# Scaled queries and keys on their way through DRAM: the four rows of a feature side by side, in place of four separate blocks

## The chip, the cores and the metric

The kernel runs on one core of one Trainium2 chip. Its time is the device time of one execution in microseconds. Three runs of the kernel before took 1242.01, 1244.40 and 1241.99 us; their median, 1242.01 us, is the number that the change is compared with.

## The reference, cut to what matters

```python
def _attn_ref(q, k, v, a_re, a_im):           # 4 batches, 8 heads, 768 steps, 48 features
    mag = np.sqrt(a_re * a_re + a_im * a_im)
    scale = np.minimum(mag, 0.999) / (mag + 1e-06)
    a_re_n, a_im_n = (a_re * scale, a_im * scale)
    for t in range(S):
        new_re = ar * S_re - ai * S_im
        new_im = ar * S_im + ai * S_re
        S_re, S_im = (new_re + k_t (outer) v_t, new_im)
        y[:, :, t] = q_t @ S_re
def _moe_ref(x, ...):    # 3072 tokens, 384 -> 1536 -> 384
    g = x @ w_gate
    return (g / (1 + np.exp(-g)) * (x @ w_val)) @ w_out
def _moe2_ref(x, ...):   # 384 -> 2048 -> 384
    h = x @ w_in
    return (h - np.tanh(h)) @ w_out
```

A recurrence with a complex decay per feature and step is followed by two feed-forward layers. All inputs of the first part are float32; the weights of the two layers are float64.

## The kernel before, in words

The recurrence is done in 24 units of 128 steps (4 batches, 6 pieces each), two units to a group. `group_steps` builds the products of the decays of a group (the tile `PL`, by chains of `cstep` on VectorE), writes them as factors into `NW`, and passes the group's last products through DRAM (`lam_d`). In front of it, `put_a` transposes the decays on TensorE into the PSUM tile `psA`, of which there is one, and ScalarE copies that into `PL` and `A0`.

`unit_a` (L367 to L402) prepares one unit. It transposes queries and keys on TensorE (`psQ`, L377), so that a partition is a feature: 3 blocks of 128 features (index j) by 128 steps. VectorE multiplies both with the real and the imaginary factors (L386) into the tile `QK`. For each of 384 features there are then four rows of 128 float32: i is 0 for the query and 1 for the key, c is 0 for the real and 1 for the imaginary factor. The scores need another grouping: for each head, 96 partitions, the 48 features of the head with the real factor and then the same 48 with the imaginary one. Getting there means moving data between partitions, and the kernel does it by way of DRAM: one write of `QK` to `qk_d` (L388), then four reads (L393): two for the keys into the tile `TK`, two for the queries into `TQ`. The four rows of a feature lie in four separate blocks of `qk_d`, 384 x 128 numbers each, so every piece that lies together in DRAM and in SBUF alike is one row: 512 bytes.

`unit_b` (L412 to L483) finishes a unit: scores `psS` from `TK` and `TQ` (L430), masked into `SC`; the state `psG` to `Z` and `Hn`, with a swap of two halves by DMA (`Zs`); the output `psY` from `SC` and, in all but the first unit of a batch, from `Hn` and `TQ` (L458, L462); and its copies into `x`, which are the tokens of the first layer. `window` interleaves `unit_b` of one unit with `unit_a` of the next.

The first layer runs in ten token tiles of two or three units (`moe1_tile`): matmuls of gate and value weights (L574), Silu on ScalarE (L578), a product and a split into two parts on VectorE (L583, L534), and the matmuls back (L558). `bg` calls let the recurrence of the following units run between its steps. Its float64 weights are loaded (L181 to L187) into two buffers `raw` and taken apart by `words` (L144 to L148) while the first tile runs. The second layer (`moe2_tile`) follows after all units are done.

Within each engine, the order of the program is set by the framework's scheduler when the kernel is built: it plays the program through with its own durations and places every instruction. All DMAs are issued by one queue, SyncE's, in that order: a DMA whose input is not ready holds up those behind it. `QK` and `TK` have one buffer (`bufs=1`), and so has `TQ` by its pool.

Of the kernel before, what the change touches and what calls it, by code (L numbers as in the profile page):

```python
# [8 lines left out]
F32 = mybir.dt.float32  # L9
# [4 lines left out]
ALU = mybir.AluOpType  # L14
# [3 lines left out]
P = 128  # L18
# [23 lines left out]
def tile_kernel(ctx: ExitStack, tc: tile.TileContext, q, k, v, a_re, a_im, w_gate, w_val, w_out, w2_in, w2_out, out):  # L42
    nc = tc.nc
    PE, ACT, DVE, POOL, SP = nc.tensor, nc.scalar, nc.vector, nc.gpsimd, nc.sync
    B, H, S, D = q.shape
    NT, DM = out.shape
# [3 lines left out]
    NJ = DM // P  # L50
    D2 = 2 * D
    G = 2
    units = [(b, c) for b in range(B) for c in range(NC)]
    NU = len(units)
# [19 lines left out]
    dram = ctx.enter_context(tc.tile_pool(name="scratch", bufs=1, space=DRAM))  # L74


    ident = const.tile([P, P], F32, name="ident")
# [20 lines left out]

    wo_d = dram.tile([NF1, P, 2, DM], F32, name="wo_d")
    lam_d = dram.tile([NU // G, DM, 3, G], F32, name="lam_d")  # L100
    qk_d = dram.tile([NU, 2, 2, DM, P], F32, name="qk_d")
    o_d = dram.tile([P, 2, NJ, NT], F32, name="o_d")
    x_d = dram.tile([NT, DM], F32, name="x_d")

# [3 lines left out]
    a1 = att.enter_context(tc.tile_pool(name="a1", bufs=1, side="right"))  # L108
# [23 lines left out]
    def PA(name):  # L132
        pool, tag = banks[0]
        banks.append(banks.pop(0))
        return pool.tile([P, 512], F32, tag=tag, name=name)

    def heads(x):
        return x.rearrange("p (h d) -> p h d", h=H)
# [228 lines left out]
    def unit_a(u):  # L367


        qn, kn = st.pop(("q", u)), st.pop(("k", u))  # L370
        NW, LS, g = st["w", u]
        W = [NW[:, c, g] for c in range(3)]
        qk = a1.tile([P, 2, NJ, P], F32, tag="qk", name="qk")
        for i, x in enumerate((qn, kn)):
            ps = PA("psQ")
            for j in range(NJ):
                PE.transpose(ps[:, P * j:P * (j + 1)], x[:, P * j:P * (j + 1)], ident)  # L377
            p = ps[:, 0:DM].rearrange("p (j t) -> p j t", j=NJ)
            near, far = (slice(0, HALF), slice(HALF, P))[::1 - 2 * i]
            DVE.tensor_tensor(out=qk[:, i, :, near], in0=p[:, :, near], in1=W[2][:, :, near], op=ALU.mult)  # L380
            ACT.copy(out=qk[:, i, :, far], in_=p[:, :, far])
            yield
        QK = a1.tile([P, 2, 2, DM], F32, tag="QK", name="QK", bufs=1)
        sh = [P, 2, DM]
        for i in range(2):
            DVE.tensor_tensor(out=QK[:, i], in0=qk[:, i].rearrange("p j t -> p (j t)").unsqueeze(1).to_broadcast(sh), in1=NW[:, 0:2, g].rearrange("p c j t -> p c (j t)"), op=ALU.mult)  # L386
        d = qk_d[u]
        SP.dma_start(out=d.rearrange("i c (j p) t -> p i c j t", p=P), in_=QK.rearrange("p i c (j t) -> p i c j t", j=NJ))  # L388
        TK = a1.tile([D2, H, P], F32, tag="TK", name="TK", bufs=1)
        TQ = a1.tile([D2, H, P], F32, tag="TQ", name="TQ")  # L390
        for i, x in ((1, TK), (0, TQ)):
            for c in range(2):
                SP.dma_start(out=x[c * D:(c + 1) * D], in_=d[i, c].rearrange("(h d) t -> d h t", h=H))  # L393
        yield
        Kn = a1.tile([P, H, 2, D], F32, tag="Kn", name="Kn")
        for c in range(2):
            ps = PA("psK")
            for j in range(NJ):
                PE.transpose(ps[:, P * j:P * (j + 1)], QK[:, 1, c, P * j:P * (j + 1)], ident)
            ACT.copy(out=Kn[:, :, c, :], in_=heads(ps[:, 0:DM]))  # L400
            yield
        st["u", u] = (Kn, TK, TQ)  # L402

# [8 lines left out]
    def unit_b(u):  # L412
        b, c = units[u]
        NW, LS, g = st["w", u]
        Kn, TK, TQ = st["u", u]
        vn = vp[u % 2]
# [10 lines left out]
        for hh in range(2):  # L427
            ps = PA("psS")
            for i in range(4):
                PE.matmul(ps[:, P * i:P * (i + 1)], lhsT=TK[:, 4 * hh + i], rhs=TQ[:, 4 * hh + i], start=True, stop=True)  # L430
            t = a1.tile([P, 4, P], F32, tag=f"SC{hh}", name="SC")
# [23 lines left out]
        for i in range(H // 2):  # L455
# [3 lines left out]
            if c > 0:  # L459
                for h in (2 * i, 2 * i + 1):  # L460
                    r = HALF * (h % 2)
                    PE.matmul(ps[r:r + D, i], lhsT=Hn[:, D * h:D * (h + 1)], rhs=TQ[:, h], start=False, stop=True)  # L462
        y = a1.tile([P, 4, 2, P], F32R, tag="y", name="y")
# [21 lines left out]
    def window(b, a):  # L485
        first = a == 1

        b = unit_b(b) if b is not None else iter(())
        a = unit_a(a) if a is not None else iter(())

        for s_ in (a, a, a, b, b, b, b, b, a, a) if first else (a, b, b, a, a, b, a, b, a, b):
            if next(s_, 0) is None:
                yield
        for s_ in (b, a):
            for _ in s_:
                yield
# [284 lines left out]
    with tc.If(bad > 0):  # L781
        with ExitStack() as gen:
# [12 lines left out]
            with tc.For_i(0, q.shape[2], TB) as t0:  # L795
# [40 lines left out]
                for i in range(2):  # L836
                    ps = PA("psY")[0:B * H, 0:n * D]
# [5 lines left out]
        with ExitStack() as gen:  # L843
# [14 lines left out]
            with tc.For_i(0, NT, P) as t0:  # L858
# [3 lines left out]
                ps = PA("psX")  # L862
# [4 lines left out]
                for f in range(NF1):  # L867
                    ps = []
                    for w in (gw, vw):
                        p = ps_1.tile([P, 512], F32, tag="l1", name="l1")[:, 0:P]  # L870
# [6 lines left out]
                for j in range(NJ):  # L877
                    p = ps_2.tile([P, 512], F32, tag="l2", name="l2")[:, 0:P]
# [4 lines left out]
                for f in range(NF2):  # L883
                    p = ps_1.tile([P, 512], F32, tag="l1", name="l3")[:, 0:P]
# [3 lines left out]
                p = ps_2.tile([P, 512], F32, tag="l2", name="l4")[:, 0:DM]  # L888
# [35 lines left out]
```

## Time and profile before

| | |
|---|---|
| median of three runs | 1242.01 us |
| profiled execution, its own time | 1243.92 us |
| span in its profile | 1241.9 us, so 2.0 us lie around the span |
| TensorE matmul busy | 1100.0 us, 89% of the span |
| VectorE busy | 988.9 us, 80% |
| ScalarE busy | 685.4 us, 55% |
| GpSimd busy | 129.8 us, 10% |
| DMA packets | 303408, of which under 512 bytes 158016 |
| DMA queue of the program, share of 16 engines | 54.9% |
| chain that ended last | PE 54%, DVE 19%, DMA 10%, ACT 10%, SPq 3% |

The shares are means over stages that differ: the first 118 us are spent before the first matmul of the first layer, the recurrence and that layer then run side by side until about 820 us, and the rest is the second layer. A "busy" share of DMA is that of 16 engines, counted by the packets that they have in hand, and can be a little over 1 in a short stretch. In the chain, SPq is time of SyncE's issuing.

### The profile page before, as it was taken

What the parts mean: (1) busy time and instruction counts of PE and PEld (TensorE: products, weight loads), DVE (VectorE), ACT (ScalarE), POOL (GpSimd) and SP (SyncE); (2) the same over time, 40 slices, a digit from 0 to 9 for tenths busy, and PEclk for the clock granted to TensorE, in tenths of its full rate; (3) what the DMA queues carried; (4) which work ended last, traced back from release to release, by engine and by line L of the source; (5) the groups of instructions that cost most, each with busy time, mean ns of one, the idle gap of its engine ahead of it and who ended that gap; (6) DMA issues with size and microseconds to landing.
All of it is one profiled execution on the core that took longest, in us unless ns stands there. A gap on an engine that the chain in (4) does not pass through costs nothing.

```text
span 1241.9 us, 20979 instructions
## 1 busy us (share of the span) xinstructions
PE 1100.0 (89%) x7440; PEld 1053.0 (85%) x7440; DVE 988.9 (80%) x2255; ACT 685.4 (55%) x1430; POOL 129.8 (10%) x110
## 2 busy tenths in 40 slices
PE   3257857889989898998999999988999999999997
PEld 1135857888988898988999999988999999999997
DVE  4878979877978768696785438899898898888986
ACT  5446537466474554547445225566666666566664
POOL 0011323212221112021110000000000000000000
PEclk9568977999999999999999999999999999999999
DMA  6397778888986979688687757751100101101000
GB/s 154 75 212 165 175 157 199 226 211 202 220 211 165 238 189 197 156 223 184 158 207 174 193 122 261 257 184 64 58 26 33 58 1 58 39 20 58 1 20 22
DMA packets 303408, 172.97 MB, mean 139 GB/s; under 512 B 158016, under 2 KB 284352, under 8 KB 303296
## 3 DMA queue, kind: packets, MB, share of 16 engines
q1 hardware_dynamic: 303296, 171.55, 54.9%
q8 instruction: 61, 1.00, 0.4%
q14 instruction: 51, 0.42, 0.1%
HBM read 121.26 MB, written 37.86 MB: 128 GB/s over the span
## 4 chain that ended last, share of the span: by engine, by line
PE 54%; DVE 19%; DMA 10%; ACT 10%; SPq 3%; issue 3%; DVEq 0%; ACTq 0%
PE l L638 15%; PE l L656 15%; PE l L574 11%; PE acc L558 5%; DVE prod L274 3%; DMA TQ<-qk_d 3%; PE psS L430 2%; DVE PL L276 2%; DVE lo L534 2%; ACT NW L323 1%; PE psG L442 1%; ACT NW L322 1%; DVE PL L277 1%; DMA lam_d<-lam 1%; DMA wo<-wo_d 1%
## 5 line engine op out<-in xcount | busy, mean ns | idle before, releaser
L574 PE MATMUL l<-x,wgv 128*128 128x256 f32 (+1 forms) x2160 | 358.8, 314 | 20.0 <-ACT t L578 15.5
L574 PEld LDWEIGHTS l<-x,wgv 128*128 128x128 f32 x2160 | 319.5, 194 | 28.1 <-ACT t L578 19.5
L656 PE MATMUL l<-x,wi 128*128 128x384 f32 x1152 | 222.9, 338 | 6.3 <-DVE t L604 6.3
L656 PEld LDWEIGHTS l<-x,wi 128*128 128x128 f32 x1152 | 202.2, 189 | 7.9 <-DVE t L604 7.6
L533 ACT CAST hi<-t 128x384 fp32r<-128x384 f32 (+1 forms) x248 | 118.9, 480 | 134.4 <-DVE t L583 100.6
L558 PE MATMUL acc<-hi,wo 128*128 128x256 f32 (+1 forms) x720 | 178.5, 314 | 3.9 <-ACT wo L154 1.5
L638 PE MATMUL l<-w,hi 128*128 128x384 f32 x768 | 177.7, 337 | 0.0
L534 DVE TENSOR_TENSOR lo<-t,hi 128x384 fp32r<-128x384 f32 (+1 forms) x248 | 133.0, 537 | 37.1 <-ACT hi L533 36.9
L638 PEld LDWEIGHTS l<-w,hi 128*128 128x128 f32 x768 | 138.6, 188 | 0.0
L558 PEld LDWEIGHTS acc<-hi,wo 128*128 128x128 f32 x720 | 127.2, 195 | 6.9 <-ACT hi L533 2.4
L597 ACT ACTIVATE t<-l 128x384 f32<-128x384 f32 x128 | 63.3, 494 | 123.9 <-PE l L656 103.6
L638 PE MATMUL l<-w,lo 128*128 128x384 f32 x384 | 110.6, 338 | 0.7 <-DVE lo L534 0.6
L558 PE MATMUL acc<-lo,wo 128*128 128x256 f32 (+1 forms) x360 | 109.7, 313 | 1.1 <-DVE lo L534 1.0
L274 DVE TENSOR_TENSOR prod<-PL 128x384 f32<-128x384 f32 x168 | 103.2, 614 | 2.6
L599 DVE TENSOR_TENSOR l<-l,t 128x384 f32<-128x384 f32 x128 | 72.3, 565 | 35.3 <-ACT uu L598 34.5
L583 DVE TENSOR_TENSOR t<-t,l 128x256 f32<-128x256 f32 (+1 forms) x120 | 56.2, 468 | 51.6 <-PE l L574 33.8
L578 ACT ACTIVATE t<-l 128x256 f32<-128x256 f32 (+1 forms) x120 | 51.2, 427 | 81.5 <-PE l L574 76.7
L600 ACT ACTIVATE vv<-uu,gbias 128x384 f32<-128x384 f32 x128 | 80.0, 625 | 2.7
L430 PE MATMUL psS<-TQ,TK 96*128 96x128 f32 x384 | 57.3, 300 | 26.5 <-DMA TQ<-qk_d 21.6
L430 PEld LDWEIGHTS psS<-TQ,TK 96*128 96x128 f32 x384 | 52.6, 211 | 30.3 <-issue 26.1
L604 DVE COPY_PREDICATED t<-far,l 128x384 f32<-128x384 int32 x128 | 75.8, 592 | 2.4
L638 PEld LDWEIGHTS l<-w,lo 128*128 128x128 f32 x384 | 70.2, 188 | 2.0 <-DVE lo L534 1.9
(128 smaller groups left out, 1701.9 us busy)
## 6 DMA issues: line engine op xcount, KB each, us to landing
wo<-wo_d SPq DMA_DIRECT2D x108, 384.0 KB, 4.2
qk_d<-QK SPq DMA_DIRECT2D x24, 768.0 KB, 5.4
raw<-in_moe_w_out_dram SPq DMA_DIRECT2D x28, 384.0 KB, 3.5
TK<-qk_d SPq DMA_DIRECT2D x48, 192.0 KB, 4.0
TQ<-qk_d SPq DMA_DIRECT2D x48, 192.0 KB, 5.3
x<-o_d SPq DMA_DIRECT2D x16, 576.0 KB, 5.2
x<-y SPq DMA_DIRECT2D x48, 144.0 KB, 5.0
raw<-in_moe_w_in_dram SPq DMA_DIRECT2D x16, 384.0 KB, 4.5
```

The lines of the kernel that those rows point to most:

```text
L274: DVE.tensor_tensor(out=pr, in0=prev.unsqueeze(2).to_broadcast(sh), in1=cur.unsqueeze(1).to_broadcast(sh), op=ALU.mult)
L430: PE.matmul(ps[:, P * i:P * (i + 1)], lhsT=TK[:, 4 * hh + i], rhs=TQ[:, 4 * hh + i], start=True, stop=True)
L533: ACT.copy(out=hi, in_=t)
L534: DVE.tensor_tensor(out=lo, in0=t, in1=hi.bitcast(F32), op=ALU.subtract)
L558: PE.matmul(acc[j], lhsT=w[:, a, j * P:(j + 1) * P], rhs=m[b], start=(f == 0 and i == 0), stop=(f == NF1 - 1 and i == 2))
L574: PE.matmul(p, lhsT=w[a][:, kk], rhs=x[b][:, kk, 0:n_t], start=(n == 0), stop=(n == 3 * NJ - 1))
L597: ACT.activation(out=t, in_=p, func=AF.Tanh)
L599: DVE.tensor_tensor(out=p, in0=p, in1=t, op=ALU.subtract)
L600: ACT.activation(out=vv, in_=uu, func=AF.Square, scale=1.0 / G_C, bias=gbias)
L604: DVE.copy_predicated(out=t, mask=far, data=p)
L638: PE.matmul(acc[tb], lhsT=g[a][:, tb * P:(tb + 1) * P], rhs=w2_hl[f][:, b], start=(f == 0 and n == 0), stop=(f == NF2 - 1 and n == 2))
L656: PE.matmul(p, lhsT=wi_hl[a][:, kk, sl], rhs=x[b][:, kk, :], start=(n == 0), stop=(n == 3 * NJ - 1))
```

## The change

`qk_d` gets the order feature, c, i, step, so that the four rows of a feature lie side by side: 2 KB. The tile `QK` gets the order j, c, i, step, which is the same within a feature; the product on VectorE (L386) writes its rows in these places. The write has one piece of 2 KB for each partition and j. The reads are two instead of four, one for each c, and bring query and key of a feature together in a piece of 1 KB, into one tile `TQK` with one buffer in place of `TK` and `TQ`. The scores and `psY` read slices of it. The transposes of `psK` read their block of `QK` at its new place. From here on lines of the kernel after are one lower than those before.

```diff
-    qk_d = dram.tile([NU, 2, 2, DM, P], F32, name="qk_d")
+    qk_d = dram.tile([NU, DM, 2, 2, P], F32, name="qk_d")
...
-        QK = a1.tile([P, 2, 2, DM], F32, tag="QK", name="QK", bufs=1)
-        sh = [P, 2, DM]
+
+        QK = a1.tile([P, NJ, 2, 2, P], F32, tag="QK", name="QK", bufs=1)
+        sh = [P, 2, NJ, P]
         for i in range(2):
-            DVE.tensor_tensor(out=QK[:, i], in0=qk[:, i].rearrange("p j t -> p (j t)").unsqueeze(1).to_broadcast(sh), in1=NW[:, 0:2, g].rearrange("p c j t -> p c (j t)"), op=ALU.mult)
-        d = qk_d[u]
-        SP.dma_start(out=d.rearrange("i c (j p) t -> p i c j t", p=P), in_=QK.rearrange("p i c (j t) -> p i c j t", j=NJ))
-        TK = a1.tile([D2, H, P], F32, tag="TK", name="TK", bufs=1)
-        TQ = a1.tile([D2, H, P], F32, tag="TQ", name="TQ")
-        for i, x in ((1, TK), (0, TQ)):
-            for c in range(2):
-                SP.dma_start(out=x[c * D:(c + 1) * D], in_=d[i, c].rearrange("(h d) t -> d h t", h=H))
+            DVE.tensor_tensor(out=QK[:, :, :, i].rearrange("p j c t -> p c j t"), in0=qk[:, i].unsqueeze(1).to_broadcast(sh), in1=NW[:, 0:2, g], op=ALU.mult)
+        SP.dma_start(out=qk_d[u].rearrange("(j p) c i t -> p j c i t", p=P), in_=QK)
+        TQK = a1.tile([D2, H, 2, P], F32, tag="TQK", name="TQK", bufs=1)
+        for c in range(2):
+            SP.dma_start(out=TQK[c * D:(c + 1) * D], in_=qk_d[u][:, c].rearrange("(h d) i t -> d h i t", h=H))
+        TQ, TK = TQK[:, :, 0], TQK[:, :, 1]
         yield
...
-                PE.transpose(ps[:, P * j:P * (j + 1)], QK[:, 1, c, P * j:P * (j + 1)], ident)
+                PE.transpose(ps[:, P * j:P * (j + 1)], QK[:, j, c, 1], ident)
```

Since the scheduler places every instruction anew, the order changes on all engines. Three places follow, all around the fourth unit (number 3), whose `psS` stands at 163 us in the trace below.

SyncE's queue from the write of this unit's `QK` on, before (`raw` are weights being loaded, `vp` the values, `x<-y` outputs on their way to the tokens):

```order
L388 DMA qk_d<-QK 128x12x128
L230 DMA vp_100<-in_v_dram 128x8x48
L393 DMA TK<-qk_d 48x8x128 x2
L393 DMA TQ<-qk_d 48x8x128 x2
L186 DMA raw<-in_moe_w_gate_dram 96x3x128
L476 DMA x<-y 48x6x128 x2
```

And after:

```order
L388 DMA qk_d<-QK 128x3x512
L186 DMA raw<-in_moe_w_gate_dram 96x3x128
L187 DMA raw<-in_moe_w_gate_dram 32x3x128
L186 DMA raw<-in_moe_w_val_dram 96x3x128
L187 DMA raw<-in_moe_w_val_dram 32x3x128
L230 DMA vp_100<-in_v_dram 128x8x48
L181 DMA raw<-in_moe_w_out_dram 128x384
L391 DMA TQK<-qk_d 48x8x256 x2
L475 DMA x<-y 48x6x128 x2
```

The write has 3 pieces a partition in place of 12, the reads are two in place of four, and five loads of weights now stand between the write and the reads.

TensorE from the last matmul of this unit's `psY` on, before (`l_` are gate and value matmuls of the first layer, `psQ` the transposes of the next unit, `psA` those of the next group's decays):

```order
L462 MATMUL psY<-TQ,Hn 48x128 x2
L574 MATMUL l_1862<-x,wgv_148 128x256 x2
...
L377 MATMUL psQ<-ident,q 128x128 x3
L574 MATMUL l_1874<-x,wgv_148 128x256 x2
...
L377 MATMUL psQ<-ident,k 128x128 x3
L264 MATMUL psA<-ident,ar 128x128 x3
L558 MATMUL acc<-hi,wo 128x256
```

And after:

```order
L461 MATMUL psY<-TQK,Hn 48x128 x2
L557 MATMUL acc<-hi,wo 128x256
...
L377 MATMUL psQ<-ident,q 128x128 x3
L557 MATMUL acc<-hi,wo 128x256 x3
L377 MATMUL psQ<-ident,k 128x128 x3
L573 MATMUL l_1886<-x,wgv_150 128x256 x2
...
L573 MATMUL l_1998<-x,wgv_128 128x256 x2
...
L264 MATMUL psA<-ident,ar 128x128 x3
```

Before, two `l` tiles of nine matmuls each stand between `psY` and the first `psA`; after, there are four such tiles and 27 `acc` matmuls (9 before the second `psQ` group, 18 behind it).

ScalarE from the copies of this unit's scores (`SC`) on, before (`dt<-raw` begins the taking apart of a loaded weight, `NW` and `PL` are the group's factors and products):

```order
L433 COPY SC<-psS 128x512
L433 COPY SC<-psS 128x512
L533 CAST hi<-t 128x256
L578 ACTIVATE t<-l_1836 128x256
L144 ACTIVATE dt<-raw 128x768
L464 CAST y<-psY 128x4x128
L144 ACTIVATE dt<-raw 128x384
L154 CAST wgv<-dt 128x768
L322 COPY NW<-PL 128x6x64
```

And after:

```order
L144 ACTIVATE dt<-raw 128x768
L577 ACTIVATE t<-l_1824 128x256
L144 ACTIVATE dt<-raw 128x384
L432 COPY SC<-psS 128x512
L154 CAST wgv<-dt 128x768
L432 COPY SC<-psS 128x512
L154 CAST wo<-dt 128x384
...
L463 CAST y<-psY 128x4x128
L144 ACTIVATE dt<-raw 128x384
...
L322 COPY NW<-PL 128x6x64
```

The first step on the `w_out` weights (128x384) has moved from behind this unit's output to ahead of its scores, and a further one stands behind the output.

## Rows read from the trace of the kernel before

**Rows 1.** Stages: length, then busy us (instructions) per engine, clock, DMA share, GB/s.

```profile
118.00:155.00 37.00, 33.67 (x274) 31.64 (x275) 34.63 (x70) 22.72 (x49) 12.16 (x7) 0.96 0.78 180
155.00:186.00 31.00, 17.11 (x124) 16.41 (x124) 21.90 (x55) 11.95 (x22) 7.47 (x6) 0.72 0.73 159
186.00:217.00 31.00, 24.39 (x156) 22.14 (x156) 28.76 (x64) 22.71 (x47) 10.33 (x6) 0.78 0.80 198
217.00:248.00 31.00, 27.04 (x233) 25.36 (x232) 25.84 (x71) 14.89 (x34) 8.58 (x7) 1.00 0.84 228
248.00:496.00 248.00, 224.00 (x1926) 213.37 (x1926) 194.09 (x463) 141.28 (x300) 45.79 (x35) 0.98 0.86 203
496.00:745.00 249.00, 240.85 (x1766) 232.40 (x1765) 159.38 (x377) 113.61 (x225) 31.76 (x28) 0.99 0.74 177
820.00:1242.00 422.00, 407.72 (x2319) 404.50 (x2317) 370.51 (x814) 256.29 (x555) 0.00 (x0) 0.99 0.12 40
```

**Rows 2.** TensorE's waits, whole span: us in total, times, longest.

```profile
PE psS L430 <- DMA TQ<-qk_d: 21.6, 9, 7.0
```

**Rows 3.** TensorE's waits, 118 to 248 us.

```profile
PE psA L264 <- ACT A L268: 10.3, 2, 9.3
PE psS L430 <- DMA TQ<-qk_d: 7.4, 4, 4.6
```

**Rows 4.** TensorE's waits, 248 to 745 us.

```profile
PE psS L430 <- DMA TQ<-qk_d: 7.2, 4, 2.7
```

**Rows 5.** Stages of 1 to 3 us, columns as in rows 1; the last two are DMA.

```profile
73.00:74.00 1.00, 0.00 (x0) 0.00 (x0) 1.00 (x3) 0.00 (x0) 0.00 (x0) 0.56 1.00 302
81.00:84.00 3.00, 0.00 (x0) 0.00 (x0) 3.00 (x7) 0.38 (x2) 0.00 (x0) 0.50 1.19 177
85.00:86.00 1.00, 0.63 (x3) 0.66 (x4) 1.00 (x4) 0.00 (x0) 0.00 (x0) 0.50 1.15 349
```

**Rows 6.** DMA issues of the page: KB each, median us to landing.

```profile
qk_d<-QK SPq DMA_DIRECT2D x24, 768.0 KB, 5.4
TK<-qk_d SPq DMA_DIRECT2D x48, 192.0 KB, 4.0
TQ<-qk_d SPq DMA_DIRECT2D x48, 192.0 KB, 5.3
```

**Rows 7.** The chain that ended last, 70 to 186 us: start, us, what.

```profile
79.59 5.64 DMA TQ<-qk_d
...
151.08 5.85 DMA qk_d<-QK
...
158.35 4.44 DMA TQ<-qk_d
...
173.14 4.04 DMA raw<-in_moe_w_out_dram
```

**Rows 8.** TensorE in order of time, 157 to 194 us.

```profile
163.00 3.75 PE L430 MATMUL psS<-TQ,TK 96*128 96x128 f32 x16 [4.57 <-DMA TQ<-qk_d]
...
185.20 0.90 PE L264 MATMUL psA<-ident,ar 128*128 128x128 f32 x3 [9.32 <-ACT A L268]
```

**Rows 9.** SyncE's queue in order of time, 60 to 172 us.

```profile
72.05 2.27 SPq L187 DMA_DIRECT2D raw<-in_moe_w_val_dram  x1
...
157.88 0.94 SPq L393 DMA_DIRECT2D TQ<-qk_d  x2
```

**Rows 10.** Waits of SyncE's queue, whole span.

```profile
SPq L186 <- DVE dt L148: 32.5, 4, 19.6
SPq L393 <- DMA qk_d<-QK: 21.7, 13, 3.0
SPq L393 <- PE psS L430: 1.7, 1, 1.7
```

**Rows 11.** VectorE by line and form: busy us, mean ns of one, idle before.

```profile
L386 DVE TENSOR_TENSOR QK<-qk,NW 128x768 f32<-128x768 f32 x48 | 47.0, 987 | 7.1 <-ACT qk L381 5.2 <-DMA qk_d<-QK 1.9
L468 DVE TENSOR_TENSOR y<-psY,y 128x512 fp32r<-128x512 f32 x24 | 16.4, 685 | 10.4 <-ACT y L464 5.3 <-DMA Zs<-Z 2.3 <-DMA wo<-wo_d 2.2
```

## The prediction, made before the change was run

> **What bounds the kernel now.** I read the busy time by stages first [rows 1]. The reader is to see three kinds of stage. From 820 us on only the second layer is left: 422 us that the change doesn't touch. From 248 to 745 us TensorE is busy 224.0 of 248 and 240.9 of 249 us, so 24.0 + 8.2 = 32.2 us is all that any shorter wait could give there. Between 118 and 248 us it is different: TensorE is busy 33.7 of 37, 17.1 of 31, 24.4 of 31 and 27.0 of 31 us, 27.8 us idle, and in the two middle stages its granted clock is 0.72 and 0.78: parts of them ran at 1.2 in place of 2.4 GHz. There a shorter wait can turn into time.
>
> Then TensorE's waits. Over the whole span the scores wait 21.6 us for the reads of `qk_d`, in 9 waits, the longest 7.0 [rows 2]; 7.4 us of it in 4 waits lie between 118 and 248 us [rows 3] and 7.2 us in 4 between 248 and 745 us [rows 4], which leaves one, of 7.0 us, earlier. The largest wait of all between 118 and 248 us is not for `qk_d`: the transposes of the decays wait 10.3 us for ScalarE, 9.3 of it in one piece [rows 3].
>
> The chain of waits shows how the two hang together [rows 7]. The write of unit 3 takes 5.85 us from issue to landing, the last of its reads 4.44; TensorE starts the scores at 163.00 after 4.57 us of waiting [rows 8]. A load of `w_out` weights is issued at 173.14, lands after 4.04 us and is taken apart on ScalarE, whose group work stands behind it, and only at 185.20 can the transposes of the next group begin, after 9.32 us in which TensorE had nothing else in front [rows 7, 8].
>
> **The change part by part.** Its own execution took 1243.92 us: 1241.9 of span and 2.0 around it, 1.9 above the median of 1242.01. I make the sum against 1243.9 and take 1.9 off at the end.
>
> Pieces. A unit has 128 x 12 = 1536 pieces in the write and 4 x 48 x 8 = 1536 in the reads; after, 128 x 3 = 384 of 2 KB and 2 x 48 x 8 = 768 of 1 KB. Over 24 units 73,728 become 27,648.
>
> The write. In a stretch that holds hardly anything but the write of unit 0, the 16 DMA engines are fully busy at 302 GB/s; the best short stretch near it, with larger pieces among its transfers, has 349 [rows 5]. The unit's 786,432 bytes take 2.6 us at the one and 2.25 at the other: 0.35 us less, of 5.4 from issue to landing [rows 6].
>
> The reads. While the reads of unit 0 and then the write of unit 1 are under way, engines that are counted as more than full (1.19) move 177 GB/s [rows 5]. By that rate a unit's reads take 4.4 us. Pieces of 1 KB from this buffer are not in the trace. Bounds: nothing gained, if the slowness comes from the place in DRAM and not from the pieces, and 2.2 us gained, if they reach 349 GB/s. I take 1.5, nearer to the fast row, since bytes per piece double. Two issues fall away: two cost 0.94 us [rows 9]. So the last read of a unit can land by 0.35 + 1.5 + 0.94 = 2.8 us sooner after its product is ready; bounds 0.9 (the issues alone) and 3.5.
>
> *Unit 0*, a wait of 7.0 us, whose last read takes 5.64 us [rows 2, 7]. Up to 2.8 us come off. What is late next is VectorE, busy 34.6 of 37 us in the stage after it [rows 1]: I count half, -1.5 (bounds 0 and -3).
>
> *118 to 248 us*: waits of 7.4 us in all, 4.6 of them at unit 3 [rows 3]. At unit 3, SyncE's order now has five loads of weights between write and reads. Their issues fit beside the 5.85 us of the write. Their data, 2 x 128 x 384 gate and value weights and 128 x 384 of `w_out` of 8 bytes each, is 1.18 MB, which takes 3.4 us at 349 GB/s, in front of the reads and only in part beside the write. So of 2.8 us I count 1.5 there, and half of the 2.8 us of the other three waits: together -3 (bounds 0 and -7).
>
> *The stall of 9.3 us.* On TensorE, four tiles of `l` matmuls and 27 of `acc` stand in front of that transpose now, where two tiles stood. On ScalarE the first step of that `w_out` load stands ahead of the scores, since its DMA is issued ahead of the reads; the 4.04 us of the chain at 173.14 should go. But another `w_out` load follows in its place, and the added matmuls need Silu from the same ScalarE. Bounds: 0 and -9.3. I take -4: what the load alone costs in the chain.
>
> *248 to 745 us*: waits for `qk_d` 7.2 us, the most that can go. TensorE is busy 93% there, and what it doesn't do now it does a little later: -1 (bounds -7 and +2, for the order moves there too).
>
> Costs of nothing. The product on VectorE writes three runs of 128 where it wrote 384 in one: nearest row, the subtraction of L468, with four runs of 128, 685 ns for 512 numbers against 987 for 768 [rows 11]. Per number that is 1.34 against 1.29 ns, so 48 x 768 x 0.05 ns = 2 us at most over all units, beside VectorE's idle time; if that cover is gone, up to 2 us. Transposes and scores read runs of 128 as before. `TQK` has one buffer, so the keys' read now waits for `psY` of the unit before, as the queries' read did; the queue waited 21.7 us for the write, and on the scores it waited once, 1.7 us [rows 10], so the write is what is late there, and keys and queries were issued back to back: 0. Behind the write, the queue's next issue took 2.27 us in place of 0.47 [rows 9], and with a quarter of the pieces this should go; it lies beside the wait for the write's landing, so 0.
>
> Sum: -1.5 - 3 - 4 - 1 = -9.5; 1243.9 - 9.5 = 1234.4, and by the median 1232.5.
>
> By the Trainium skill, "DMA: Bandwidth & Descriptors", section Specifications, 512 bytes is the least transfer for line rate. By this rule pieces of 512 bytes are at line rate already and longer ones bring nothing; the write's 302 GB/s is near that, the reads' 177 is not [rows 5]. By the rule the sum would keep the issues and the order alone, which is the first rival.
>
> **The rivals.**
>
> 1. *The pieces cost nothing, and the stall moves.* Reads no faster; what is left is 0.94 us of issuing on five waits, half of it hidden, and 2 us of the stall, the other `w_out` load taking the rest: -4.5, so 1237.5. For it: the same DRAM is read, and transfers wait for each other wherever the engines are full. Against it: 177 beside 349 GB/s at full engines.
>
> 2. *All of it is given back.* The waits shrink by 5 us, and VectorE, at 34.6 of 37 and 28.8 of 31 us [rows 1], sets the pace of the first 250 us anyway; later TensorE is full. Then -1 to 0: 1241.5. Against it: in the chain of unit 3 VectorE has hardly a part [rows 7], and its stage 155 to 186 us has VectorE at 21.9 of 31.
>
> 3. *Slower: a load of weights holds up the reads.* SyncE's queue is in order. At unit 3 five loads stand in front of the reads, into buffers that VectorE must have emptied. Such loads waited on L148 in the trace: 32.5 us in 4 waits, 8.1 each [rows 10]. If the buffer comes free later than the write lands (5.85 us after its issue), the excess delays the reads, the scores, and everything that stands behind them on TensorE. One wait of 8.1 us in full, begun as the write lands, plus 2 us for matmuls at 1.2 GHz behind a longer idle stretch: +10, so 1252. For it: order and rows both show it possible. Against it: L148 stands just behind the unit's product on VectorE.
>
> That the pieces don't get longer is excluded by the shapes in the order: 512 numbers in the write, 256 in the reads.
>
> **How the numbers follow.** The forecast has a chance of 0.52, with 1224 to 1236 as its own range (below, half the way from its sum to that of all lower bounds, -26; above, a sum of -6); the first rival 0.13, the second 0.17, the third 0.18. A difference under 0.2%, 2.5 us, can't be told from none: faster is below 1239.5, slower above 1244.5. Faster: 0.52 + 0.13 = 0.65, and 0.02 of the second rival, whose edge reaches over: 0.67. The same: 0.14. Slower: 0.18, and 0.01 of the second: 0.19. Range: below, three quarters of the way to all lower bounds, 1219, since the gains of one cause come together. Above, it takes in the second rival and part of the third: 1247.
>
> **What would show it.** The packets of the program's queue should fall by 73,728 - 27,648 = 46,080. The write should land in about 5 us, the reads in 4 to 4.5 at the median, though each carries twice the bytes. TensorE's wait for the reads should fall from 21.6 to about 12 us. In the stages from 118 to 248 us, idle time of TensorE should fall from 27.8 to about 20 us; after 248 us nothing should move by over 3 us. The prediction is wrong if the reads of `TQK` land later after the product than before, if SyncE waits for L148 in front of them, or if a new wait of several us stands in front of TensorE between 150 and 250 us.

## The result and the profile after

The changed kernel takes 1257.13 us, the kernel before 1242.38 us (medians of four runs each): a ratio of 1.0113, 95% interval [1.009, 1.0137]. It is 1.1% slower. The forecast was 1232.5 us, with 1219 to 1247 as its range, so the sign was wrong, and the range too. The profiled execution took 1254.98 us, with a span of 1253.3 us. Two single executions of kernels further below, at a granted clock of 0.56 and 0.74 in place of 0.95, are left out of the medians and ratios there.

The stages of the kernel after, with the columns of [rows 1]:

```profile
118.00:155.00 37.00, 30.11 (x217) 29.06 (x218) 31.59 (x57) 21.48 (x45) 8.85 (x7) 0.86 0.65 148
155.00:186.00 31.00, 23.21 (x207) 21.08 (x206) 28.35 (x69) 11.17 (x22) 5.97 (x5) 0.94 0.83 188
186.00:217.00 31.00, 19.69 (x125) 17.88 (x124) 24.20 (x63) 26.30 (x53) 6.93 (x4) 0.83 0.73 210
217.00:248.00 31.00, 25.97 (x205) 25.07 (x206) 25.61 (x67) 9.71 (x23) 6.26 (x6) 0.87 0.76 206
248.00:496.00 248.00, 222.85 (x1895) 213.82 (x1894) 182.12 (x443) 139.65 (x297) 39.82 (x34) 0.95 0.80 195
496.00:745.00 249.00, 235.82 (x1729) 227.50 (x1730) 171.89 (x392) 117.66 (x232) 38.38 (x32) 0.99 0.76 183
820.00:1253.00 433.00, 418.21 (x2377) 414.30 (x2375) 381.91 (x843) 263.09 (x569) 0.00 (x0) 0.99 0.14 46
```

TensorE is idle for 37 + 3 x 31 - 98.98 = 31.0 us between 118 and 248 us (27.8 before), for 25.2 us in the next stage (24.0) and for 13.2 in the one after (8.2). The last row begins at the same 820 us as in [rows 1] and is 11 us longer, with 10.5 us more of matmuls: the work of the first layer that is still left there is what the earlier stages lost.

TensorE's waits over the whole span (us in total, times, longest):

```profile
PE psS L429 <- DMA TQK<-qk_d: 28.9, 9, 7.0
```

From 118 to 248 us:

```profile
PE l L573 <- ACT t L577: 16.0, 8, 4.2
PE psS L429 <- DMA TQK<-qk_d: 6.0, 3, 2.8
...
PE psA L264 <- ACT A L268: 1.1, 1, 1.1
```

From 248 to 745 us:

```profile
PE psS L429 <- DMA TQK<-qk_d: 16.4, 5, 7.0
```

The scores wait 28.9 us for the reads, not 21.6 [rows 2]; all of the growth lies behind 248 us, where 7.2 us became 16.4 [rows 4]. The stall of 9.3 us [rows 3] is gone, as forecast: 10.3 us of waiting for `A` became 1.1. But the gate and value matmuls now wait 16.0 us for Silu (`t`, L577). In the same stretch of the kernel before it was 5.6 us:

```profile
PE l L574 <- ACT t L578: 5.6, 6, 1.5
```

The DMAs of the page (KB each, median us to landing):

```profile
qk_d<-QK SPq DMA_DIRECT2D x24, 768.0 KB, 4.9
TQK<-qk_d SPq DMA_DIRECT2D x48, 384.0 KB, 6.2
```

And the queue's packets, MB and share of 16 engines:

```profile
q1 hardware_dynamic: 256448, 171.55, 53.6%
```

The write lands after 4.9 us (5.4 in [rows 6]), the reads after 6.2 us each. The kernel before had 303296 packets in this queue, so 46,848 went.

The chain that ended last, at unit 3 (start, us, what):

```profile
163.62 8.71 DMA TQK<-qk_d
```

TensorE there in order of time, the wait in brackets:

```profile
167.65 3.66 PE L573 MATMUL l<-x,wgv 128*128 128x256 f32 x18 [4.21 <-ACT t L577]
172.47 2.02 PE L429 MATMUL psS<-TQK 96*128 96x128 f32 x16 [1.15 <-DMA TQK<-qk_d]
```

And SyncE's queue ahead of it:

```profile
158.27 0.38 SPq L388 DMA_DIRECT2D qk_d<-QK  x1
...
163.05 1.04 SPq L391 DMA_DIRECT2D TQK<-qk_d  x2
```

The reads are issued 4.8 us behind the write, so the queue did not wait for L148 in front of them. The last of them lands 8.71 us after its issue, where [rows 7] had 4.44. TensorE's new wait there, 4.21 us, is for Silu.

### The profile page after: what moved, and what is told of

It reads as the page before. It is cut to its first block, busy times and chain, and to the rows that moved or that the text cites. A ratio compares the mean times of both kernels' runs of the same rounds, so it can differ in the third digit from the quotient of the medians.

```text
span 1253.3 us, 20885 instructions
## 1 busy us (share of the span) xinstructions
PE 1101.9 (88%) x7440; PEld 1057.2 (84%) x7440; DVE 991.7 (79%) x2255; ACT 687.0 (55%) x1430; POOL 118.3 (9%) x110
## 4 chain that ended last, share of the span: by engine, by line
PE 58%; DVE 16%; DMA 11%; ACT 8%; issue 3%; SPq 2%; DVEq 0%; ACTq 0%
PE l L637 15%; PE l L655 15%; PE l L573 14%; PE acc L557 6%; DMA TQK<-qk_d 4%; PE psS L429 3%; DVE prod L274 2%; DMA qk_d<-QK 2%; DMA raw<-in_moe_w_val_dram 1%; DVE PL L276 1%; DVE lo L533 1%; PE psY L457 1%; PE psG L441 1%; DVE QK L387 1%; PE psY L461 1%
## 5 line engine op out<-in xcount | busy, mean ns | idle before, releaser
L573 PE MATMUL l<-x,wgv 128*128 128x256 f32 (+1 forms) x2160 | 365.7, 317 | 28.3 <-ACT t L577 23.5
L573 PEld LDWEIGHTS l<-x,wgv 128*128 128x128 f32 x2160 | 324.9, 198 | 35.2 <-ACT t L577 27.1
L577 ACT ACTIVATE t<-l 128x256 f32<-128x256 f32 (+1 forms) x120 | 51.2, 427 | 78.8 <-PE l L573 75.1
L429 PE MATMUL psS<-TQK 96*128 96x128 f32 x384 | 61.3, 313 | 31.6 <-DMA TQK<-qk_d 28.9
L429 PEld LDWEIGHTS psS<-TQK 96*128 96x128 f32 x384 | 56.7, 224 | 34.6 <-issue 31.3
```

The lines of the kernel that those rows point to most:

```text
L573: PE.matmul(p, lhsT=w[a][:, kk], rhs=x[b][:, kk, 0:n_t], start=(n == 0), stop=(n == 3 * NJ - 1))
```

## Experiments

Two things changed together: the DMAs with their tile, and the order of every engine's instructions, which the scheduler made anew. In the kernels below an order is imposed: `keep_order` ties each engine's instructions to the order that they had in a kernel already profiled, without adding a wait. Lines are shifted by the added code (L456, or L455 with joined reads, is `psS` where it was L430). Ratios are to the kernel before on the same chip, with 95% intervals; they are not the quotients of the medians given here. Code is cut to the lines that matter.

**One part alone.** First the new DMAs in the old order; the two reads stand at the place of the queries' reads, the later of the two pairs.

```diff
+    keep_order(nc, tc)
```

This one line, with the table of the order of before (left out here), is added to the changed kernel.

> The write, the reads and the tile of the kernel after, with every engine's instructions kept in the order of the kernel before (the two reads stand where the queries' two reads stood). Theory A, the transfers: reads of 1 KB out of rows of 2 KB are no faster, each issue lands later (6.2 us against 4.0 and 5.3 before), and the scores wait for them whatever the order: 1250 to 1260 us, near the kernel after, and the scores' wait for the reads stays at 25 to 30 us. Theory B, the order: the scheduler's new order causes the loss, the transfers are worth a little: 1236 to 1242 us, with a wait for the reads under 21 us.

Measured: 1253.30 us, 1.0049 [1.0023, 1.0076]. On this chip the kernel before took 1246.46 us, so the ratio lies between the two theories. TensorE's largest wait, whole span:

```profile
PE psS L455 <- DMA TQK<-qk_d: 31.0, 15, 7.2
```

> The write of 512-byte pieces, the four reads and the two tiles of the kernel before, with every engine's instructions in the order of the kernel after (each of the two reads is replaced by a pair). Theory A, the transfers: the new order by itself costs nothing, 1238 to 1245 us. Theory B, the order: 1252 to 1262 us, with Silu's share in TensorE's waits between 118 and 248 us at 12 us or more, as in the kernel after (16.0), where the kernel before has 5.6.

Measured, for the DMAs of before in the changed kernel's order: 1264.24 us, 1.0160 [1.0134, 1.0185]. TensorE's largest wait in it, whole span:

```profile
PE psS L456 <- DMA TQ<-qk_d: 33.6, 10, 7.7
```

Both parts cost, the order more; together they give 1.0113, so the new DMAs fit the order that was made for them better than the old ones do.

**The place in DRAM.** Rows of 1 KB in two blocks, so that what a read takes lies together, in the old order:

```diff
-    qk_d = dram.tile([NU, DM, 2, 2, P], F32, name="qk_d")
+    qk_d = dram.tile([NU, 2, DM, 2, P], F32, name="qk_d")
```

> DRAM order c, feature, i, step: pieces of 1 KB in the write and in the two reads, and each read's rows lie without gaps; all instructions in the order of the kernel before. If reads of the kernel after are slow because they take half of each 2 KB row, these reads land sooner (4.5 to 5.5 us at the median in place of 6.2) and the time is 1236 to 1243 us. If pieces of 1 KB from this buffer are slow wherever they lie, it equals new_dma_old_order within 3 us.

The tile, the write and the reads follow this order (left out here). Measured: 1255.32 us, 1.0082 [1.0051, 1.0113]; the reads land after 6.4 us, and after 6.3 us in the run with rows of 2 KB in the same order. The place is not what slows them.

**The exchange by itself.** A kernel that does nothing but move such tiles (the rest of the computation is left out, here and in the next two): a write, the reads, and an operation on VectorE that waits for them.

> Nothing of the reference is computed: zeros are written to the output, and one exchange after another (a write of 768 KB from SBUF to DRAM and the reads back to 96 partitions) runs six times with nothing else on the DMA engines, each in one of these DRAM orders: four blocks (512-byte pieces), rows of 2 KB (2 KB out, 1 KB in), the same rows read in 512-byte pieces, two blocks (1 KB both ways), rows of 2 KB at a pitch of 2304 bytes, and at a pitch of 4096 bytes, last a read of 64 partitions with 8 KB each. Theory A says by its place: reads of rows of 2 KB take as long as those of four blocks or longer (over 4.5 us to the last landing), two blocks or the padded pitch take 1 us less. Theory B says alone on the engines the 1 KB reads land 1 us or more before the 512-byte reads: packets decide, and the kernel after lost by its order.

VectorE's waits in one round of it (the time in brackets is the wait):

```profile
80.77 0.29 DVE L40 TENSOR_TENSOR X<-T 96x128 f32<-96x128 f32 x1 [8.21 <-DMA T<-blk]
90.73 0.29 DVE L40 TENSOR_TENSOR X<-T 96x128 f32<-96x128 f32 x1 [9.67 <-DMA T<-fea]
```

The forms with two blocks, and with rows of 2 KB at a pitch of 2304 or 4096 bytes, took 9.4 to 10.0 us, as the rows of 2 KB did: the place in DRAM made no difference here either. But 8.2 us for four blocks and 9.7 for rows of 2 KB: I read this as reads of 1 KB being slower, and split them up:

> Nothing but the exchange's reads, one form after the other with a wait between them, six times over: the write of rows of 2 KB alone; then reads of the same 768 KB as two DMAs of 1 KB pieces (the change), four DMAs of 1 KB pieces (four heads each), eight of 1 KB pieces (two heads each), four DMAs of 512-byte pieces (before), two DMAs of 512-byte pieces, eight of 512-byte pieces, and two DMAs of 512-byte pieces for the keys alone, half the bytes. In the first run of the exchange alone, two DMAs of 1 KB pieces took about 1.9 us longer than four of 512 bytes. Theory A, the number of DMAs: fewer DMAs in flight are slower, so two of 512 bytes take about as long as two of 1 KB (6 us), and four and eight of 1 KB take 4.2 us or less, like four of 512 bytes. Theory B, the size of the piece: all forms with 1 KB pieces take about 6 us, however many DMAs, and all forms with 512-byte pieces about 4.2 us. Theory C, the bytes of one DMA on its way by themselves: 384 KB in one DMA takes longer to start or to end than 192 KB, so forms order by the size of one DMA, eight being the fastest.

This run showed that the reading was wrong. The waiting operation read only the queries of two heads; where keys and queries, or heads, come by different DMAs, it waited for some of them only. Two DMAs of 512-byte pieces, where it had to wait for all, took 6.1 us, no less than two of 1 KB. So once more, with an operation that reads all heads, keys and queries:

> The exchange by itself again, this time with a wait on VectorE that reads all heads and both of query and key, so that it ends with the last read. In the two runs of the exchange and the reads alone, the waiting operation read only part of the tile, and where the reads were split by query and key, or by heads, it waited for some of them only; so 8.0 against 9.6 us, and 4.2 against 6 us, may compare half a transfer with a whole one. Theory A, the piece: with the full wait, four reads of 512 bytes still take about 4.2 us and two of 1 KB about 6 us, and the exchange 8.0 against 9.6 us. Theory B, the bytes: the reads of 768 KB take about 6 us in every form, whatever the piece and the number of DMAs (the two DMAs of 512-byte pieces, for which the earlier wait was whole, took 6.1 us beside 5.9 us for two of 1 KB); then the exchange in blocks takes 10 us or more, and rows of 2 KB come out a little shorter, by the 0.3 to 0.6 us of the write and of two issues.

One round, in this order: the exchange by blocks; by rows with two reads; by rows with four reads; then reads alone: two of 1 KB pieces, four and eight of 1 KB, four, two and eight of 512 bytes, and at last the keys alone. Six of the ten lines are shown.

```profile
109.61 0.29 DVE L39 TENSOR_TENSOR X<-T 96x128 f32<-96x128 f32 x1 [9.62 <-DMA T<-ubk]
119.51 0.29 DVE L39 TENSOR_TENSOR X<-T 96x128 f32<-96x128 f32 x1 [9.61 <-DMA T<-fea]
129.13 0.29 DVE L39 TENSOR_TENSOR X<-T 96x128 f32<-96x128 f32 x1 [9.33 <-DMA T<-fea]
135.27 0.29 DVE L39 TENSOR_TENSOR X<-T 96x128 f32<-96x128 f32 x1 [5.85 <-DMA T<-fea]
...
153.05 0.29 DVE L39 TENSOR_TENSOR X<-T 96x128 f32<-96x128 f32 x1 [5.75 <-DMA T<-fea]
...
169.41 0.29 DVE L39 TENSOR_TENSOR X<-T 96x128 f32<-96x128 f32 x1 [3.71 <-DMA T<-fea]
```

Theory B holds. The medians of the rounds (six of each form; the first wait of the run, which also contains its beginning, left out): blocks 9.62, rows with two reads 9.55, rows with four reads 9.24 us; reads alone 5.35 to 6.12 us over all pieces and numbers, and 3.73 for half the bytes. At the same number of DMAs 1 KB pieces are at most 0.4 us shorter (four: 5.35 against 5.75). The change also halved the number, and its two DMAs of 1 KB pieces are, at 5.88, even a little longer than the four of 512 bytes before.

**Rows of 2 KB, but four reads.**

```diff
-        TQK = a1.tile([D2, H, 2, P], F32, tag="TQK", name="TQK", bufs=1)
...
+        TK = a1.tile([D2, H, P], F32, tag="TK", name="TK", bufs=1)
+        TQ = a1.tile([D2, H, P], F32, tag="TQ", name="TQ")
+        for i, x in ((1, TK), (0, TQ)):
+            for c in range(2):
+                SP.dma_start(out=x[c * D:(c + 1) * D], in_=qk_d[u][:, c, i].rearrange("(h d) t -> d h t", h=H))
```

> Half of the change: written in rows of 2 KB, but read in four DMAs of 512 bytes into separate tiles for keys and queries, every engine's instructions in the order of before. If the two joined reads are what costs 0.5% in the old order (keys and queries arrive together, the scores wait for 384 KB DMAs), this runs in 0.996 to 1.001 of before: the write is shorter and the reads are as they were. If it is the rows of 2 KB in DRAM or the product's strided output that cost, it is slower by about 0.5%, as with all of the change's DMAs in this order.

Measured: 1238.59 us, 0.9973 [0.9955, 0.9992]: slightly faster than before. TensorE waits 16.7 us in 7 waits for the queries' reads. And the scheduler, left free, gives this kernel the order of before on all five engines (built, not run). So rows of 2 KB neither cost anything nor move anything; what is left of the change is the joined reads and their tile. The same kernel once more, on the chip of the next experiment:

> The kernel with rows of 2 KB written and four reads of 512 bytes once more, beside the one-tile form on the same chip. The exchange by itself was 0.4 us shorter than that of before (9.24 against 9.63 us), and TensorE waits for some nine of the 24, so I expect 0.995 to 0.999 again; 1.000 or above would make the first result a matter of chance.

Measured: 1238.12 us, 0.9982 [0.9961, 1.0003]. The gain of about 0.2% is at the edge of what these runs can tell.

**The shared buffer.** What do two tiles have that one hasn't? SyncE's queue at unit 11 of the kernel before shows it:

```profile
391.18 0.37 SPq L388 DMA_DIRECT2D qk_d<-QK  x1
...
395.93 0.32 SPq L393 DMA_DIRECT2D TK<-qk_d  x1
...
405.39 0.38 SPq L393 DMA_DIRECT2D TQ<-qk_d  x1
```

And TensorE's last matmuls of `psY` of the unit before:

```profile
404.88 0.42 PE L462 MATMUL psY<-TQ,Hn 96*48 96x128 f32 x4
```

The keys are read 4.75 us after the write is issued, the queries 14.2 us after it, when `psY` of the unit before has read `TQ`. Keys don't have to wait for that: `TK` is read by the scores alone. In one tile with one buffer they do. So this kernel has four reads as the last one, and the same order, but its keys and queries are halves of one tile:

```diff
-        TK = a1.tile([D2, H, P], F32, tag="TK", name="TK", bufs=1)
-        TQ = a1.tile([D2, H, P], F32, tag="TQ", name="TQ")
+        TQK = a1.tile([D2, 2, H, P], F32, tag="TQK", name="TQK", bufs=1)
+        TQ, TK = TQK[:, 0], TQK[:, 1]
```

> Rows of 2 KB written and four reads of 512 bytes, as in the kernel that ran in 0.997 of before, and in the same order; but keys and queries are two halves of one tile with one buffer, as in the change, so the keys' reads must wait until the output matmuls of the unit before have read their queries. Nothing else differs. Theory A, the shared buffer: in the old order the change's joined reads cost 0.5% against before and 0.8% against the four reads because the keys can no longer be read early; then this kernel gives up the same, 1.002 to 1.008 of before, with the keys' first read issued just behind the last psY in the units where it came earlier. Theory B, two DMAs of 384 KB in pieces of 1 KB are themselves slower than four: then this kernel stays at 0.996 to 0.999.

Measured: 1254.75 us, 1.0121 [1.0090, 1.0153]. Theory A holds, and the buffer costs more than I gave it. The largest wait of SyncE's queue in front of these reads, whole span:

```profile
SPq L419 <- PE psY L488: 20.1, 7, 10.1
```

The queue at unit 11:

```profile
397.20 0.37 SPq L414 DMA_DIRECT2D qk_d<-QK  x1
...
399.83 0.57 SPq L475 DMA_DIRECT2D Zs<-Z  x1
411.38 0.32 SPq L419 DMA_DIRECT2D TQK<-qk_d  x1
```

And TensorE there:

```profile
410.92 0.43 PE L488 MATMUL psY<-TQK,Hn 96*48 96x128 f32 x4
...
420.25 0.55 PE L584 MATMUL acc<-hi,wo 128*128 128x256 f32 x1 [5.96 <-DMA wo<-wo_d]
```

The first of these three views is a wait that the queue didn't have with two tiles: 20.1 us in 7 waits for `psY`, the longest 10.1. At unit 11 the queue issues nothing between 400.4 and 411.38, just as `psY` ends. Behind the waiting read stand the `wo` loads of the first layer, and TensorE then waits 5.96 us for one of them.

Where this is paid shows in two stretches, with the columns of [rows 1]: first the kernel with two tiles (this execution took 1236.67 us), then that with one (1264.22 us), then the changed kernel's first stretch.

```profile
118.00:290.00 172.00, 140.94 (x1108) 132.07 (x1107) 146.96 (x332) 95.08 (x198) 48.21 (x31) 0.90 0.80 199
290.00:745.00 455.00, 430.55 (x3391) 413.83 (x3392) 319.31 (x763) 232.35 (x475) 68.42 (x56) 0.98 0.76 190
118.00:290.00 172.00, 139.50 (x1074) 131.31 (x1075) 143.16 (x323) 93.69 (x196) 47.91 (x29) 0.88 0.76 192
290.00:745.00 455.00, 415.62 (x3266) 398.13 (x3261) 317.24 (x761) 228.80 (x470) 68.79 (x57) 0.97 0.74 184
118.00:290.00 172.00, 133.26 (x1027) 126.35 (x1028) 138.40 (x320) 95.44 (x196) 35.73 (x29) 0.88 0.77 191
```

TensorE is idle for 31.1 and 24.4 us with two tiles, for 32.5 and 39.4 with one: the shared buffer costs 1.4 us up to 290 us and 15 us behind it. The queue of before agrees: up to unit 8 the queries' reads are issued at most 2.4 us behind the keys', and unit 9, at 341 us, is the first with a larger gap, 6.4 us. But the changed kernel is idle for 38.7 us in the first stretch already. The shared buffer doesn't explain that part of the loss. Nor does it explain the order there: left free, the scheduler gives the kernel with one tile and four reads the order of before on every engine up to the reads of unit 9 (built, not run), while the changed kernel's order differs at unit 3 already. What is left as the source of the early order is the joining of the reads into two DMAs.

The changed kernel itself avoids that blockage, by its order. Its queue at unit 11:

```profile
400.27 0.37 SPq L388 DMA_DIRECT2D qk_d<-QK  x1
...
408.60 4.77 SPq L541 DMA_DIRECT2D wo<-wo_d  x3
...
414.72 0.44 SPq L391 DMA_DIRECT2D TQK<-qk_d  x1
```

And the queue's wait for `psY` there, whole span:

```profile
SPq L391 <- PE psY L461: 1.9, 1, 1.9
```

The scheduler has put both reads behind the other DMAs, so in the whole run the queue waits for `psY` only once, 1.9 us. The price is a read of 768 KB that begins 14.5 us after the write, where the keys' half began after 4.75.

**The order.** Where does the new order lose? With the DMAs of before, the new order was imposed up to a cut near 290 us, and the old one behind it; and the reverse. On each engine the cut is a place where both orders have issued the same set of instructions.

> The DMAs of before; the order of the changed kernel in the stretch up to about 290 us of the trace (on each engine up to a place where both orders have issued the same set of instructions), and the order of before from there on. The new order in full cost 1.6%, 20 us, with these DMAs. Theory A: the loss is made where the orders differ most, between 120 and 290 us, with Silu and the reads as the waits; then this kernel is 1.0 to 1.7% slower than before. Theory B: the loss is spread over the many small differences behind 290 us, where the scheduler put the reads and the scores anew for each unit; then this kernel is within 0.4% of before.

Measured: 1253.82 us, 1.0095 [1.0067, 1.0124].

> The complement of the order cut at 290 us: the DMAs of before, the order of before up to about 290 us, the order of the changed kernel from there on. The full new order cost 1.6% with these DMAs and its first part alone 0.95%. If the two parts add, this kernel is 1.004 to 1.009; if the first part carries it all and its combination with the rest is what made 1.6%, this is within 0.2% of before.

Measured: 1250.52 us, 1.0071 [1.0045, 1.0097]. The parts add up to the whole: 0.95 + 0.71 = 1.66% beside 1.60%. TensorE's waits from 118 to 290 us, of the first of the two:

```profile
PE l L600 <- ACT t L604: 14.6, 10, 3.9
PE psS L456 <- DMA TQ<-qk_d: 12.5, 4, 6.8
...
PE psA L290 <- ACT A L294: 1.1, 1, 1.1
```

They are the waits of the changed kernel (16.8 us for Silu, 13.0 for the reads and 1.1 for `A` there), without its DMAs: where the stall on `A` went, Silu and a wait of 6.8 us for the reads stand. The kernel before has 8.2, 8.6 and 11.1. Last, the third rival's cause, the loads of weights ahead of the reads: in the full new order, again with the DMAs of before, those of units 0 to 4 go behind the reads on SyncE's queue.

> The DMAs of before in the order of the changed kernel, but on SyncE's queue the loads of weights that stand between the write of a unit and its reads (units 1 to 4, five of them at unit 3) go behind the reads. If the loads in front of the reads are what costs, as in my third rival, then most of the 1.6% of the new order goes: 1.000 to 1.007 of before. If the cost is the place of the matmuls, Silu and the recurrence on TensorE, ScalarE and VectorE, then it stays at 1.012 to 1.018.

Measured: 1271.21 us, 1.0229 [1.0199, 1.0259], 0.7% worse than the 1.0160 with the loads in front (measured on another chip). TensorE's waits, whole span:

```profile
PE l L600 <- ACT t L604: 28.7, 14, 9.9
PE psS L456 <- DMA TQ<-qk_d: 25.4, 8, 6.4
...
PE acc L584 <- ACT wo L180: 9.7, 3, 8.6
```

The reads gain 33.6 - 25.4 = 8.2 us against the same order with the loads in front, but a wait of 9.9 us for Silu and one of 8.6 for `wo`, which is made from the loaded weights, take more. So loads in front of the reads do delay them, and putting them behind wins nothing back.

## Why the prediction was wrong

**The step that failed** is the price of the new order. The prediction took -4 for the stall that the order removes, named what stands against it, "the added matmuls need Silu from the same ScalarE", without a number, and put the stages behind 248 us at -1, with +2 as the most that the order could cost there. Measured with the DMAs of before, the new order alone costs 1.60%, some 20 us: 0.95% up to 290 us, near 12 us, and 0.71% behind it, near 9 us. The stall of 9.3 us went, as forecast and for more than the 4 us taken. But between 118 and 248 us 5.6 us of waiting for Silu became 16.0, which is the whole gain of the stall and more. The order makes the sign. These waits are only a part of what it costs: from 118 to 290 us the waits for `A`, Silu and the reads are 27.9 us before and 30.9 after, of 32.6 and 38.7 us in which TensorE is idle; the rest is spread over smaller waits.

**The second step** is a term that was put at nothing: "the keys' read now waits for `psY` of the unit before, as the queries' read did; ... keys and queries were issued back to back: 0." They were back to back at unit 3, the place of [rows 9], and up to unit 8. At unit 11 9.5 us lie between the first of the keys' reads and the first of the queries'. The total of waits in [rows 10] did not show it, because the queue didn't wait there: other DMAs had been put in between. With the order and the DMAs of rows and four reads held, the shared buffer alone takes the ratio from 0.9982 to 1.0121, measured on one chip: 1.4%, some 17 us, nearly all of it behind 290 us. The changed kernel doesn't pay this as a blocked queue but by reads that are issued later; how much of its loss behind 290 us is the buffer's, no run shows.

**The reads' 1.5 us** were a mis-sized term. I took the 177 GB/s of [rows 5] for a price of short pieces and the 349 for what long ones reach, and the lower bound, nothing, was the truth for the reads as the change joins them. The sum of 2.8 us for a unit (write 0.35, reads 1.5, issues 0.94) measures 9.62 - 9.55 = 0.07 us by itself. Rows with four reads, whose pieces are those of before, give 9.62 - 9.24 = 0.38 us, and the two joined reads give 0.31 of it back. The 0.94 us of [rows 9] that two issues take were thus no price either: the other reads are under way meanwhile, and 768 KB in eight DMAs took no longer than in two.

**The write** was right: forecast to land in about 5 us, it lands after 4.9, in the same kernel that lost.

**The rivals.** The first was right about the pieces, and only about them. The third gave 1252 us, the nearest time, but by luck: its wait for L148 didn't come in front of the reads. In the kernel with one tile and four reads a wait for a buffer does hold up the queue, on `psY`, not on the weights; in the changed kernel that is 1.9 us in all. The packets fell nearly as worked out, 46,848 against 46,080. The range's lower end, three quarters of the way from -9.5 to -26.3, is 1220, not 1219.

**What stays open:** which of the moved instructions costs how much in the new order. The cut at 290 us shows that it is not one place, and putting the loads of weights up to unit 4 behind the reads made it slower. Two joined reads without a shared buffer weren't run: a `TQK` with two buffers, which would take the wait away and leave the joined reads, lacks 4.3 KB a partition of room.

## What to carry to other kernels

Before joining two tiles, list the last reader of each: with one buffer the joined tile is free only when the later of them is, and its whole transfer then starts there. Look for this at every unit of the queue's timeline, not at one. Where a change makes the scheduler move every engine's instructions, give the moves that cost a number as well as those that gain: a stall that goes can come back as another wait, as 9.2 us on `A` did as 10.4 us on Silu. And a slow rate at full engines says nothing of its cause; move the same bytes in another form, by themselves, and wait for all of them, before giving longer pieces a price.

## What was not expected of the hardware

Into 48 partitions a DMA, 768 KB of reads took 5.35 to 6.12 us by themselves, in pieces of 512 bytes and of 1 KB, in two, four or eight DMAs; 384 KB took 3.73. The second half of the bytes, 393,216, thus added 5.75 - 3.73 = 2.02 us in four reads of 512 bytes against two, which is 195 GB/s as an estimate, close to the 177 of [rows 5]. No other form was measured at half its bytes; why the rate is below the write's 302 was not settled. In the first run of the exchange alone 512 KB in pieces of 8 KB, into 64 partitions, took 5.0 us.
